# Routed attention and a gated feed-forward in one kernel: a unit's filler pieces start in its first gap instead of its second

## The chip, the cores and the metric

One Trainium2 chip, one core. The time is the device time of one execution, in microseconds (us); a lower one is better. Medians are over several executions. A profile shows one execution, and its span is about 1.8 us shorter than the time of that execution. The granted clock is the share of its full speed at which TensorE was allowed to run.

## The reference, cut to what matters

```python
# attention: 4 batches, 8 heads, 768 tokens, head size 64, 16 clusters per head
mask   = argmax(q_n @ c_n) == argmax(k_n @ c_n)       # a query sees the keys of its own cluster
attn   = softmax(where(mask, q @ k.T / 8, -1e9)) @ v
x      = attn as [3072 tokens, 512]
# feed-forward
xn     = x / sqrt(mean(x*x) + 1e-6) * rms_g
out    = (silu(xn @ w_gate) * (xn @ w_val)) @ w_out   # 512 -> 1536 -> 512
```

Inputs and output are float32.

## The kernel before

The work is cut into 8 *units* of 384 query tokens. A unit has 8 heads, and each head's scores come in three pairs of matmuls, so a unit has 24 *gaps*: the places after each score pair, where TensorE can do something else while ScalarE takes the exponential of the pair. The other work is cut into *pieces*, and a list of pieces is poured into the gaps by cost:

```python
    def attention(heads, fill, skip=0, hooks={}):
        gaps = [(u, h, i) for u, h in heads for i in range(UNITS[u][2])]
        total, done, n = sum(c for c, _ in fill), 0.0, 0
        for at, (u, h, i) in enumerate(gaps):
            scores(u, h, i)                       # 2 matmuls, then the exponential on ScalarE
            if i == (0 if (u, h) == (1, 0) else 1):
                for p in due:
                    pv(*p)                        # p*v of the head before: 18 small matmuls
                due[:] = [(u, h)]
            ...
            while n < len(fill) and at >= skip and done <= total * (at + 1 - skip) / (len(gaps) - skip):
                done += fill[n][0]
                fill[n][1]()
                n += 1
        for _, f in fill[n:]:
            f()
```

The pieces of a unit, in order: the last four gate/val pairs of the unit two before it; its own predecessor's normalisation (no TensorE work); nine output pieces with four transposes of the normalised tokens woven in; then eight gate/val pairs (0 to 7), and in units 2 to 5, woven among these, the preparation of a later *group* of four heads: eight f32 transposes, casts, and the cluster steps.

```python
        of["cl"] = cluster_products(...)          # TensorE, then a transpose on VectorE
        ...                                       # largest, same, back: VectorE only
   # a piece's chain
   gate: 4 matmuls -> tanh (ScalarE) -> (th+1)*gate (VectorE)    # its PSUM buffer is free after the last
   val:  4 matmuls -> 0.5*th*val (VectorE)
   transposes: 3 matmuls -> copy (ScalarE) -> casts (GpSimd and VectorE)
```

All of these write to one pool of three PSUM buffers; the scores have two of their own:

```python
    ps_s = pool("ps_s", 2, space=PSUM)    # score pairs, two banks each
    ps_a = pool("ps_a", 1, space=PSUM)    # p*v
    ps_g = pool("ps_g", 3, space=PSUM)    # everything else, tag "gen"
```

In the lines of the profile PE is TensorE, ACT ScalarE, DVE VectorE, POOL GpSimd and PEld TensorE's weight loads. A row gives its start, its duration and what was done; `[0.23 <-DVE th L432]` at its end means that the engine stood idle for 0.23 us before it, until an instruction of VectorE on line 432 was done. L333 is the score matmuls (tile s) and, on ScalarE, L337 their exponential (pT); L351 is p*v (acc) and L356 and L358 its division on VectorE; L423 is gate and val; L431 is the tanh, L432 and L436 the multiplies of gate and val; L448 is the output pieces; L208 and L214 are the f32 transposes and their copies; L227 is the casts; L244, L249, L253 and L271 are the cluster steps on VectorE.

The softmax here doesn't subtract the row's maximum and nothing guards it: scores larger than these inputs give would overflow.

## Time and profile before

| | kernel before |
|---|---|
| median time, first three runs (lowest, highest) | 346.39 us (346.12, 346.4) |
| span of the profile | 344.5 us |
| busy: TensorE / ScalarE / VectorE / GpSimd | 98% / 75% / 64% / 33% |
| length of unit 2; 3, 4 and 5; 6 (first score pair to the next unit's) | 42.16; 41.03 to 41.04; 36.37 us |
| unit 7 and the tail (first score pair to the end of TensorE's last matmul) | 74.78 us |

The lengths are differences of start times of the first score pair of each unit in the trace. A unit of 41.03 us holds some 40.5 us of TensorE work at its floor, as the prediction adds up. Unit 2 is longer because it holds one cluster product more (0.78 us, left over from an earlier group).

### The profile page before, as it was taken

How to read it: one execution, taken by the hardware profiler on the slowest of the kernel's cores; microseconds unless marked ns; L12 is line 12 of the kernel's file. 1: busy time of each engine (PE TensorE's matmuls, PEld its weight loads, DVE VectorE, ACT ScalarE, POOL GpSimd, SP SyncE). 2: the span in 40 equal slices, each digit the busy share in tenths (PEclk: the TensorE clock that was granted, in tenths of full speed). 3: DMA queues.
4: the chain of work that ended last, by engine and by line, in shares of the span. 5: the costliest groups of instructions: out<-in, count | busy, mean ns of one | idle time of the engine just before them, and what ended most of it. 6: DMA issues, size and time to landing. Idle time of an engine off the chain costs nothing.

```text
span 344.5 us, 7999 instructions
## 1 busy us (share of the span) xinstructions
PE 337.7 (98%) x3045; PEld 208.4 (61%) x3045; DVE 220.4 (64%) x540; ACT 259.4 (75%) x449; POOL 112.8 (33%) x225
## 2 busy tenths in 40 slices
PE   8999999999999999999999999999999999999996
PEld 4547657555765567565675656755566656655654
DVE  6999796975578626785367745686356645675330
ACT  5899979856888768886797777888778877764322
POOL 6999596234336205180132702435000000000000
DMA  8999979982450014400130010000100001001002
GB/s 266 381 209 219 263 147 232 149 275 87 147 159 17 30 62 149 139 22 35 61 94 2 23 63 33 0 9 17 63 32 0 2 33 61 2 1 64 30 2 91
DMA packets 27302, 31.62 MB, mean 92 GB/s; under 512 B 4480, under 2 KB 24320, under 8 KB 27264
## 3 DMA queue, kind: packets, MB, share of 16 engines
q1 hardware_dynamic: 18608, 25.02, 22.2%
q0 software_dynamic: 8368, 5.71, 10.2%
q8 instruction: 24, 0.39, 0.5%
q10 hardware_dynamic: 288, 0.39, 0.3%
q14 instruction: 14, 0.11, 0.1%
HBM read 28.35 MB, written 6.29 MB: 101 GB/s over the span
## 4 chain that ended last, share of the span: by engine, by line
PE 88%; ACT 5%; DVE 5%; issue 1%; POOL 0%; ACTq 0%; DVEq 0%; POOLq 0%
PE gate L423 17%; PE val L423 17%; PE o L448 17%; PE s L333 16%; PE acc L351 9%; PE tq L208 4%; ACT pT L337 4%; PE sc L241 3%; PE tx L396 1%; PE warm L117 1%; DVE pads L312 1%; DVE kext L317 1%; DVE qext L317 1%; PE o L459 1%; DVE scT L308 1%
## 5 line engine op out<-in xcount | busy, mean ns | idle before, releaser
L337 ACT ACTIVATE pT<-s,off 128x768 bf16<-128x768 f32 x192 | 170.6, 904 | 34.0 <-PE s L333 32.9
L333 PE MATMUL s<-qext,kext 80*128 80x384 bf16 x384 | 94.4, 327 | 1.8 <-ACT pT L337 1.1
L432 DVE SCALAR_TENSOR_TENSOR th<-th,gate 128x384 f32<-128x384 f32 x84 | 46.3, 552 | 51.8 <-ACT th L431 51.6
L423 PE MATMUL gate<-xnT,wg 128*128 128x384 bf16 x384 | 78.6, 326 | 0.1
L423 PE MATMUL val<-xnT,wv 128*128 128x384 bf16 x384 | 78.1, 326 | 0.0
L448 PE MATMUL o<-wo,gvT 128*128 128x512 bf16 x276 | 67.6, 379 | 0.0
L227 POOL CAST qext<-qkT 64x384 bf16<-64x384 f32 x64 | 35.3, 557 | 75.4 <-ACT qkT L214 35.9
L333 PEld LDWEIGHTS <-kext 80*128 80x128 bf16 x384 | 36.6, 98 | 31.4 <-issue 6.4
L431 ACT ACTIVATE th<-gate 128x384 f32<-128x384 f32 x84 | 41.2, 490 | 13.9 <-PE gate L423 13.5
L423 PEld LDWEIGHTS <-wv 128*128 128x128 bf16 x384 | 36.1, 97 | 25.5 <-issue 3.8
L423 PEld LDWEIGHTS <-wg 128*128 128x128 bf16 x384 | 35.9, 97 | 24.5 <-issue 3.3
L436 DVE SCALAR_TENSOR_TENSOR gvT<-th,val 128x384 bf16<-128x384 f32 x84 | 46.2, 550 | 6.2 <-PE val L423 1.6
L351 PEld LDWEIGHTS <-pT 128*128 128x128 bf16 x1152 | 43.4, 97 | 10.1 <-DVE x L358 1.1
L351 PE MATMUL acc<-vbf,pT 128*128 128x65 bf16 x1152 | 45.7, 193 | 0.6 <-ACT pT L337 0.2
L448 PEld LDWEIGHTS <-gvT 128*128 128x128 bf16 x276 | 25.7, 97 | 25.5 <-issue 0.6
L208 PE MATMUL tq<-ident_f,qk 128*128 128x128 f32 x192 | 30.8, 279 | 0.0
L214 ACT ACTIVATE qkT<-tq 128x384 f32<-128x384 f32 x57 | 26.9, 495 | 3.7 <-PE tq L208 3.2
L282 POOL DMA_DIRECT2D qext<-oh x40 | 19.1, 487 | 30.6 <-DVE oh L271 24.2
L397 DVE TENSOR_SCALAR xnT<-tx,gcol 128x384 bf16<-128x384 bf16 x28 | 10.6, 413 | 28.8 <-PE tx L396 28.8
L208 PEld LDWEIGHTS tq<-ident_f,qk 128*128 128x128 f32 x192 | 23.9, 144 | 6.6 <-ACT qkT L214 1.0
L451 ACT COPY o_sb<-o 128x512 f32<-128x512 f32 x23 | 13.5, 585 | 17.7 <-PE o L448 17.7
L282 POOL DMA_DIRECT2D kext<-oh x40 | 19.1, 485 | 9.6 <-DVE oh L271 9.6
(81 smaller groups left out, 247.2 us busy)
## 6 DMA issues: line engine op xcount, KB each, us to landing
qk<-in_q_dram SPq DMA_DIRECT2D x32, 192.0 KB, 3.8
vs<-in_v_dram SPq DMA_DIRECT2D x32, 192.0 KB, 4.0
out_dram<-o_sb SPq DMA_DIRECT2D x23, 256.0 KB, 2.0
qk<-in_k_dram SPq DMA_DIRECT2D x30, 192.0 KB, 4.1
wg<-in_moe_w_gate_dram POOLq DMA_DIRECT2D x4, 384.0 KB, 8.8
wv<-in_moe_w_val_dram POOLq DMA_DIRECT2D x4, 384.0 KB, 11.7
wo<-in_moe_w_out_dram POOLq DMA_DIRECT2D x3, 512.0 KB, 7.6
qext<-oh POOLq DMA_DIRECT2D x40, 12.0 KB, 1.6
```

What stands on the lines that cost most here:

```text
L208: nc.tensor.transpose(ps[:, i * P:(i + 1) * P], qk[:, part, 2 * i:2 * i + 2].rearrange("p t d -> p (t d)"), ident_f)
L214: nc.scalar.activation(to, ps, ACT.Copy, scale=by)
L227: on.tensor_copy(to, of)
L282: on.dma_start(out=ext[D:D + NC, h, e * UQ:(e + 1) * UQ], in_=put[g, m][32 * h + e * NC:32 * h + (e + 1) * NC])
L333: nc.tensor.matmul(ps[:, j, :w] if nt == HT else flat[:, j * w:(j + 1) * w], lhsT=cols(kext[g % 4][:KR, hh], g, kc // HT, kc % HT * P, (kc ...
L337: nc.scalar.activation(pT[u, h][:, n * i:n * i + n, :w], of, ACT.Exp, bias=off, scale=scale * ZS)
L351: nc.tensor.matmul(acc[:, h % 2, t], lhsT=pT[u, h][:, kc, t * P:(t + 1) * P], rhs=vbf[g % 4][:, hh, kc % HT * 2 + kc // HT], start=kc == 0 ...
L423: nc.tensor.matmul(ps, lhsT=w[:, c, f * P:(f + 1) * P], rhs=xnT[u][:, c, :n], start=c == 0, stop=c == CC - 1)
L431: nc.scalar.activation(th, ps, ACT.Tanh, scale=0.5)
L432: nc.vector.scalar_tensor_tensor(th, th, 1.0, ps, op0=ALU.add, op1=ALU.mult)
L436: nc.vector.scalar_tensor_tensor(gvT[u][:, f, :n], gates[u], 0.5, ps, op0=ALU.mult, op1=ALU.mult)
L448: nc.tensor.matmul(outs[u], lhsT=gvT[u][:, f, t * P:(t + 1) * P], rhs=wo[:, f], start=f == 0, stop=f == FC - 1)
```

## The change

The number at the end of the call is `skip`, the gaps at the start of a unit that get no piece. The intent is that TensorE should have something to do between the first two score pairs of a unit instead of waiting there for ScalarE.

```diff
-            attention([(u, h) for h in range(H)], fill + spread(ffn[CC:CUT], group(g) if g < NG else []), 1)
+            attention([(u, h) for h in range(H)], fill + spread(ffn[CC:CUT], group(g) if g < NG else []))
```

It holds for units 2 to 7. No piece is added or removed, and their order among themselves stays. The same total is now divided among 24 gaps and not 23.

## The prediction

> **What bounds the kernel now.** I read the page first (busy shares and the chain of work that ended last), then the list of waits, then the timeline of TensorE, engine by engine, around the places that the change touches.
>
> ```profile
> PE 337.7 (98%) x3045; PEld 208.4 (61%) x3045; DVE 220.4 (64%) x540; ACT 259.4 (75%) x449; POOL 112.8 (33%) x225
> ...
> PE 88%; ACT 5%; DVE 5%; issue 1%; POOL 0%; ACTq 0%; DVEq 0%; POOLq 0%
> ```
>
> TensorE is 98% busy and carries 88% of the chain. But a busy matmul row overlaps the next one, so I counted starts, not busy time. In the timeline a score pair starts 0.33 us before what follows it, a gate or val piece (4 matmuls) 0.65 us, an output piece (4 matmuls of 512 columns) 0.86 us, the 18 matmuls of a p*v product 0.55 us. One unit with a group (units 2 to 5) holds 24 score pairs, 8 p*v, 24 gate/val pieces, 9 output pieces, 12 bf16 transposes at 0.055, 8 f32 transpose triples at 0.33 and 2 cluster products at 0.78: 7.92 + 4.40 + 15.60 + 7.74 + 0.66 + 2.64 + 1.56 = 40.5 us. The double score pairs with which units 3, 4, 5 and 6 begin start at 107.23, 148.27, 189.30 and 230.34, so such a unit takes 41.04 us. Only 0.5 us of 41 is TensorE standing still. That is the main reading: reordering can move tenths, not microseconds.
>
> Where are those tenths? The waits of TensorE for ScalarE:
>
> ```profile
> PE s L333 <- ACT pT L337: 1.1, 4, 0.3
> ```
>
> and the start of the last unit in the timeline of TensorE (start, duration, what):
>
> ```profile
> 266.06 0.81 PE L423 MATMUL val<-xnT,wv 128*128 128x384 bf16 x4
> 266.71 0.49 PE L333 MATMUL s<-qext,kext 80*128 80x384 bf16 x2
> 267.47 0.49 PE L333 MATMUL s<-qext,kext 80*128 80x384 bf16 x2 [0.26 <-ACT pT L337]
> 267.79 0.71 PE L351 MATMUL acc<-vbf,pT 128*128 128x65 bf16 x18
> ```
>
> The second pair starts 0.76 us after the first where 0.33 would do: 0.43 us lost. The two score tiles alternate, so the pair needs the exponential of the pair two before it, and nothing was put between the pairs to give ScalarE time. At the other starts the loss is smaller:
>
> ```profile
> 107.23 0.88 PE L333 MATMUL s<-qext,kext 80*128 80x384 bf16 x4
> 107.95 0.71 PE L351 MATMUL acc<-vbf,pT 128*128 128x65 bf16 x18
> ```
>
> 0.72 us instead of 0.65: 0.07 us, the same at 148.27, 189.30 and 230.34. Unit 2 (65.07) loses 0.82 - 0.65 = 0.17 there and another 0.14 before a val piece at 68.86 that waits for a gen buffer (its gate started at 68.07, 0.79 before).
>
> **What the Trainium skill says.** "TensorE: Matmul & The Clock Gate", section "Wait — 56ns, not 53.3ns?": warm start-to-start is the columns over 2.4 GHz plus about 2.5 ns, 215.7 ns at 512; for 384 columns that works out to an estimated 162.5. The trace agrees: 0.86/4 = 215 ns and 0.65/4 = 162 ns, at a granted clock of 1.0. So the matmuls are at their floor. Same page, "Architectural detail: the array is 16× 32×32, not 1× 128×128": ScalarE and VectorE are strictly first in, first out. So a gate's tanh placed between two exponentials delays the second; the trace shows tanh and exponentials in program order throughout. "Perfetto Trace Analysis", "Identifying the Most-Contended Engine", warns against matmul busy time as a measure; here the busy rows (0.81 us for a piece that costs 0.65) agree. "ScalarE: Activation LUTs", "What ACT_TABLE_LOAD costs": back-to-back activations overlap by about 93 ns; here exponentials of 0.90 us follow each other at about 0.80.
>
> **The change part by part.** A unit has 24 gaps, one after each score pair. Pieces have a cost in the list; after a gap, pieces are issued while the running sum is within total*(gaps counted)/(gaps in all). The number 1 at the end of the call left the first gap empty: 23 gaps shared the work. Without it 24 do. The total is 27.62 with a group (units 2 to 5), so the quota goes from 27.62/23 = 1.20 to 1.15 per gap; units 6 and 7 have 23.82, from 1.036 to 0.993. No instruction is added or removed, and the order of the pieces among themselves is unchanged; only the score pairs and p*v products move against them.
>
> *Removed.* A gate and a val piece (1.30 us) now lie between the first two score pairs of units 2 to 7. That covers 0.43 + 4 x 0.07 + 0.17 = 0.88 us, and with an earlier gate in unit 2 probably the 0.14 too: 1.02 us, all on TensorE's path.
>
> *Moved at the border.* VectorE is behind there (the cluster steps of the old unit end at 109.46). With the durations of the trace: first gate at 107.56, val at 108.21, second pair 108.86, p*v 109.19, next gate 109.74, next val 110.39. That val needs the buffer of the first gate: its tanh would be done at about 109.25, VectorE's multiply at about 110.0. It fits with 0.4 us to spare. The remainder of the p*v (division, 0.7 us of VectorE) comes later by two multiplies and nobody waits for it. I count 0.
>
> *Moved within the unit.* Counting the quota by hand, the same pieces come out in each gap from gap 19 on, so the 0.16 us before the last val of units 2 to 5 (106.10 to 106.59 for a pair) stays. Between gaps 12 and 18 the grouping differs. Now the trace has, from the timeline of TensorE:
>
> ```profile
> 131.85 0.49 PE L208 MATMUL tq<-ident_f,qk 128*128 128x128 f32 x3
> 132.18 0.49 PE L333 MATMUL s<-qext,kext 80*128 80x384 bf16 x2
> 132.51 0.49 PE L208 MATMUL tq<-ident_f,qk 128*128 128x128 f32 x3
> 132.92 0.81 PE L423 MATMUL gate<-xnT,wg 128*128 128x384 bf16 x4
> ```
>
> 0.41 instead of 0.33 before the gate: 0.08 us. After the change both transposes of head 1 fall into gap 14 and gate 2 and val 2 into gap 15. Gap 14 then has 0.33 + 0.33 + 0.33 = 0.99 us of TensorE but about 0.79 + 0.38 + 0.38 = 1.55 us of ScalarE (exponential and two copies). Put on a clock that starts with the pair of gap 13: ScalarE gives the copies at 4.28 and 4.66, the tanh of gate 2 at 5.83; VectorE releases val 1 at 3.95, gate 2 at 6.43, val 2 at 7.2. TensorE wants gate 2 at 3.83 (waits about 0.15), gate 3 at 6.34 to 6.5 (fits or 0.1), the second transpose of head 2 at about 7.1 (waits about 0.1). Estimate 0.25 us in the place of 0.08, in four units: 4 x 0.17 = +0.7 us. Which of the three gen buffers a piece gets is not in the code, so this term runs from 0 to 0.6 a unit. Units 6 and 7 have no transposes and only light gaps: 0.
>
> Sum: -1.02 + 0.68 = -0.34 us, 346.39 to about 346.0.
>
> **The rivals.** First, the transpose gaps cost nothing, because ScalarE's idle time in the trace (75% busy) swallows the backlog: then the 0.08 go too and the time is 346.39 - 1.02 - 0.33 = 345.0. For it: the score tiles are double and gaps 17 and 18 with three transposes between them cause no loss today. Against it: there a p*v (0.55 us) follows and here none. Second, the gen buffers become the bound: VectorE's backlog at the border makes the early gate and val wait, or the transpose gaps wait 0.6 us; then 346.39 - 1.02 + 4 x 0.5 = 347.4, more if the border waits too. For it: VectorE runs without a break from 104.46 to 110.6; against it: the 0.4 us worked out above. Third, the normalisation of the previous unit now starts one gap earlier (gap 4 instead of 5 in units 2 to 5); it needs the last p*v of that unit, issued in gap 1, and lies about 5 us behind it instead of 7, while the division ends about 2 us behind it. Nothing: 0.
>
> **Range and chances.** The middle is 346.0; the ends of the two terms give 345.0 and 347.4, both less likely than the middle, and three runs of before spread by 0.28 us. Range 345.2 to 346.9. Two per cent is 6.9 us; the whole stall budget of the six units is about 3 us, so faster by 2% is out of reach (0.005), and slower by 2% would need a stall of over 1 us in every unit (0.01).
>
> **What would show it.** Right: at the start of units 3 to 7 a pair, a gate, a val, a pair, each at 0.33/0.65/0.65; the wait of the score matmuls for the exponential gone or down to 0.4 us or less; units 3 to 5 each between 40.9 and 41.4 us long; the unit before the last gains nothing except its border; last unit 0.4 us shorter. Wrong: a gate or val at the border that waits for VectorE, or a gap 14 to 17 in which TensorE loses more than 0.6 us, or an end (from the last score pair on) that is longer than now.

## More of the kernel before

The Trainium skill, "PSUM — Partial Sum Buffer", section "Specifications (TRN2)", gives 8 banks of 512 float32 per partition. Two score tiles of two banks, one p*v bank and three gen banks are all 8; no run here tries a ninth. A fourth gen buffer would have to be taken from another tile.

## The result, and the profile after

The changed kernel took 348.28 us (median of 4, 347.92 to 348.38), the kernel before beside it 346.38 us (4 runs). The ratio is 1.0055, with a 95% interval of 1.0037 to 1.0072: slower by half a per cent, and outside the predicted range. A ratio here and below is the mean time of one kernel's runs over that of the other's of the same rounds, so not quite the ratio of the medians.

The two lines of the page of the changed kernel that answer to those shown of before (busy time; chain by engine):

```profile
PE 338.8 (98%) x3045; PEld 208.4 (60%) x3045; DVE 221.3 (64%) x540; ACT 261.1 (75%) x449; POOL 112.8 (33%) x225
...
PE 85%; DVE 8%; ACT 5%; issue 1%; POOL 0%; ACTq 0%; DVEq 0%; POOLq 0%
```

The busy shares have hardly moved, but 3% of the chain has gone from TensorE to VectorE. The list of waits (who waits for whom: us in total, times, longest) says where to look:

```profile
PE val L423 <- DVE th L432: 0.9, 4, 0.2
```

This line is new: four times a val piece waits for the multiply that belongs to a gate. The wait of the scores for the exponential has gone from 1.1 us in four waits to 0.8 in three.

**The border is as predicted.** This is TensorE at the start of the last unit after the change (timeline: start, duration, what):

```profile
269.08 0.49 PE L333 MATMUL s<-qext,kext 80*128 80x384 bf16 x2
269.41 0.81 PE L423 MATMUL gate<-xnT,wg 128*128 128x384 bf16 x4
270.06 0.81 PE L423 MATMUL val<-xnT,wv 128*128 128x384 bf16 x4
270.71 0.49 PE L333 MATMUL s<-qext,kext 80*128 80x384 bf16 x2
```

Starts are 0.33, 0.65 and 0.65 apart: nothing waits, where 0.43 us were lost before. Unit 3 starts in the same way, without a wait.

**The loss is in units 2 to 5**, the units that prepare a group. From the starts of the first score pairs:

| unit | before | after | difference |
|---|---|---|---|
| 2 | 42.16 | 42.66 | +0.49 |
| 3 | 41.03 | 41.64 | +0.61 |
| 4 | 41.03 | 41.66 | +0.63 |
| 5 | 41.04 | 41.65 | +0.60 |
| 6 | 36.37 | 36.31 | -0.07 |
| 7 and tail | 74.78 | 74.35 | -0.43 |

(The differences are taken before rounding.) To find the places I took, for each matmul, the time to the next one's start, less the usual time for that shape. In each of units 2 to 5 two places stand out that the kernel before does not have, or has with a small wait only (0.08 before gate 2). The first, in unit 3:

```profile
131.44 0.81 PE L423 MATMUL val<-xnT,wv 128*128 128x384 bf16 x4
132.09 0.49 PE L333 MATMUL s<-qext,kext 80*128 80x384 bf16 x2
132.41 0.90 PE L208 MATMUL tq<-ident_f,qk 128*128 128x128 f32 x6
133.15 0.49 PE L333 MATMUL s<-qext,kext 80*128 80x384 bf16 x2
133.74 0.81 PE L423 MATMUL gate<-xnT,wg 128*128 128x384 bf16 x4
```

This is val 1, the two transposes of head 1, and gate 2. From the score pair at 133.15 to the gate are 0.59 us, where 0.33 would do: 0.26 lost. The two transposes take 0.74 from 132.41 to 133.15 where 0.66 would do; 0.055 of this is one wait inside the second of them, and I count it with the first place, 0.31 in all. Note that no idle time is printed before gate 2. The ends of matmul rows are modelled, 0.16 us later than the next start, so a short wait shows in the starts only.

The second place is val 4, 6.5 us later (0.23 us of idle time printed, but 0.39 lost: 1.04 from the transposes' start against 0.65):

```profile
138.23 0.81 PE L423 MATMUL gate<-xnT,wg 128*128 128x384 bf16 x4
138.88 0.49 PE L333 MATMUL s<-qext,kext 80*128 80x384 bf16 x2
139.21 0.82 PE L208 MATMUL tq<-ident_f,qk 128*128 128x128 f32 x6
140.25 0.81 PE L423 MATMUL val<-xnT,wv 128*128 128x384 bf16 x4 [0.23 <-DVE th L432]
```

In the kernel before the same pieces stand in another order against the scores and p*v:

```profile
137.74 0.81 PE L423 MATMUL gate<-xnT,wg 128*128 128x384 bf16 x4
138.39 0.82 PE L208 MATMUL tq<-ident_f,qk 128*128 128x128 f32 x6
139.04 0.49 PE L333 MATMUL s<-qext,kext 80*128 80x384 bf16 x2
139.37 0.71 PE L351 MATMUL acc<-vbf,pT 128*128 128x65 bf16 x18
139.92 0.81 PE L423 MATMUL val<-xnT,wv 128*128 128x384 bf16 x4
```

There a p*v (0.55 us) lay between the transposes and val 4. Now val 4 falls into gap 18, before it. These are the pieces of the gaps concerned, by the cost list (tr1a and tr1b are the two transposes of head 1, and so on; casts left out):

| gap | before | after |
|---|---|---|
| 13 (has a p*v) | val 0, tr0b, gate 1 | tr0b, gate 1, val 1 |
| 14 | val 1, tr1a | tr1a, tr1b |
| 15 | tr1b, gate 2, val 2 | gate 2, val 2 |
| 16 (has a p*v) | tr2a, gate 3 | tr2a, gate 3, tr2b |
| 17 | tr2b, val 3 | val 3, gate 4 |
| 18 | gate 4, tr3a, tr3b | tr3a, tr3b, val 4 |
| 19 (has a p*v) | val 4, gate 5 | gate 5 |

### The profile page after: what moved, and what is told of

It reads as the page before. It is cut to its first block, busy times and chain, and to the rows that moved or that the text cites. A ratio compares the mean times of both kernels' runs of the same rounds, so it can differ in the third digit from the quotient of the medians.

```text
span 346.5 us, 8001 instructions
## 1 busy us (share of the span) xinstructions
PE 338.8 (98%) x3045; PEld 208.4 (60%) x3045; DVE 221.3 (64%) x540; ACT 261.1 (75%) x449; POOL 112.8 (33%) x225
## 4 chain that ended last, share of the span: by engine, by line
PE 85%; DVE 8%; ACT 5%; issue 1%; POOL 0%; ACTq 0%; DVEq 0%; POOLq 0%
PE o L448 17%; PE val L423 17%; PE gate L423 17%; PE s L333 15%; PE acc L351 9%; ACT pT L337 3%; PE tq L208 3%; PE sc L241 3%; DVE th L432 1%; PE tx L396 1%; DVE gvT L436 1%; DVE kext L227 1%; PE warm L117 1%; DVE pads L312 1%; DVE kext L317 1%
```

## The experiments

My first theory: the border gains some 0.9 us, and two places in each of units 2 to 5 cost 0.31 and 0.39 us. The rival: the early pieces at the border themselves disturb VectorE, and what is seen later follows from that. All kernels ran in 4 to 6 timed runs beside the kernel before (medians of it 346.40 or 346.41). All outputs are right. Before the first score pair, profiles differ by up to 0.9 us from run to run (10.0 to 11.0 us), so I compare unit lengths beside the medians.

| run | median us | ratio to before (95%) | unit 3, us |
|---|---|---|---|
| kernel before | 346.4 | 1 | 41.03 |
| changed kernel | 348.28 | 1.0055 (1.0037 to 1.0072) | 41.64 |
| first gap alone | 345.37 | 0.9972 (0.9959 to 0.9984) | 40.97 |
| regrouped, first gap empty | 350.62 | 1.0122 (1.0109 to 1.0136) | 41.95 |
| val 4 after p*v | 346.27 | 1.0000 (0.9987 to 1.0013) | 41.26 |
| transposes apart | 347.89 | 1.0047 (1.0033 to 1.0060) | 41.65 |
| cast behind val 1 | 348.16 | 1.0041* (1.0013 to 1.0069) | 41.60 |
| casts behind gate 4 | 348.07 | 1.0040* (1.0010 to 1.0070) | 41.60 |
| val 4 and cast | 346.27 | 0.9993* (0.9965 to 1.0021) | 41.21 |
| val 4, cast, val 6 first | 346.22 | 0.9985* (0.9958 to 1.0012) | 41.16 |
| late gaps alone | 349.23 | 1.0080 (1.0067 to 1.0094) | 41.72 |
| val 4 and val 1 back | 345.68 | 0.9979 (0.9967 to 0.9992) | 41.01 |
| last two units only | 345.67 | 0.9979 (0.9967 to 0.9992) | 41.03 |
| first gap alone, val 6 first | 344.50 | 0.9947 (0.9935 to 0.9960) | 40.81 |

(* With the execution of 349.52 us among those of the kernel before, hence the wide intervals. Without it the ratios of the means would be 1.0051, 1.0049, 1.0003 and 0.9994, in this order; no conclusion below changes.)

### The two halves of the change

**First gap alone.** On the kernel before, the first two pieces go to gap 0; everything else keeps its gap.

```diff
-    def attention(heads, fill, skip=0, hooks={}):
+    def attention(heads, fill, skip=0, hooks={}, early=0):
 ...
+            for cost, piece in fill[:early] if at == 0 else []:
+                done += cost
+                piece()
+                n += 1
 ...
-  ... group(g) if g < NG else []), 1)
+  ... group(g) if g < NG else []), 1, early=2)
```

> The kernel before with one thing moved: the first gate and val piece of units 2 to 7 go to the first gap instead of the second, and all other pieces stay in their gaps of before. My theory now: the border gains what the prediction said (0.07 us in units 3 to 6, about 0.2 in unit 2, 0.43 in unit 7, together about 0.9 us) and the loss of the change lies only in the regrouping of later gaps. It expects 345.4 us (345.2 to 345.7), so about 0.9 us faster than before. The rival, that the early pieces at the border themselves cost (VectorE is behind there, their gen buffers come late), expects 347 us or more.

Measured 345.37, in the middle of the expected range. Units 3 to 5 are 0.06 us shorter than before, unit 2 by 0.30, unit 7 by 0.42. The border pieces gain and cost nothing here. Gap 1 is empty in this kernel, though, where the changed kernel fills it too; so the rival is out only together with the run "late gaps alone" below, which has the losses without any piece in the first gap.

**Regrouped, first gap empty.** The changed kernel, but gap 0 gets nothing and gap 1 four pieces.

```diff
-            while n < len(fill) and at >= skip and done <= ...
+            while n < len(fill) and at >= max(skip, hold) and done <= ...      # hold=1 for units 2 to 7
```

> The changed kernel with the first gap of units 2 to 7 left empty: the second gap takes four pieces, all later gaps are as in the changed kernel. Theory (the loss is two places in each of units 2 to 5: gate 2 behind two transposes loses about 0.31 us where 0.085 was lost before, and val 4 behind two transposes about 0.39): the border gain is missing, the loss is all there: 346.38 + 4 x (0.31 + 0.39 - 0.085) = 348.8 us (348.4 to 349.2), slower than the changed kernel. The rival (the border costs): 346.4, as before.

Measured 350.62, far off. Both places are there with the same 0.31 and 0.39, but the experiment made a third: four gate/val pieces in a row in gap 1, whose second val waits for its buffer (110.91 to 111.80 where 0.65 would do). That is 0.24 us in each of units 3 to 7 and 0.47 in unit 2, most of the 1.8 us above what I expected:

```profile
110.91 0.81 PE L423 MATMUL gate<-xnT,wg 128*128 128x384 bf16 x4
111.80 0.48 PE L423 MATMUL val<-xnT,wv 128*128 128x384 bf16 x2
```

So it does not measure the regrouping by itself. I repeated it in a cleaner form.

**Late gaps alone.** The kernel before up to gap 11, the grouping of the changed kernel from gap 12 on.

```diff
+            if at == 12:
+                skip = late          # 0 in units 2 to 5, else as it was
```

> The kernel before up to gap 11 of each unit (first gap empty, second gap with two pieces), then in units 2 to 5 the grouping of the changed kernel from gap 12 on (gap 12 takes one piece more to catch up). This is the regrouping without the crowded second gap that spoilt the first attempt. Theory: the two places cost what they cost in the changed kernel: 346.4 + 4 x (0.31 + 0.39 - 0.085) = 348.9 us (348.5 to 349.3). Rival, the earlier pieces of the first half also take part: 347.5 or less.

Measured 349.23, within the expected span. Unit 3 is 0.69 us longer than before, and in its starts the same three waits stand: 0.055 and 0.257 at gate 2, and 0.389 at val 4. With the first run this splits the change: the border -1.0 us, the regrouping +2.8 us. The sum is +1.8, and +1.9 was measured.

**Last two units only.** The first gap filled only where no group is prepared.

```diff
-  ... group(g) if g < NG else []))
+  ... group(g) if g < NG else []), int(g < NG))
```

> The changed kernel with the first gap filled only in units 6 and 7, which have no transposes; units 2 to 5 as before. Theory: the borders of units 6 and 7 gain 0.07 + 0.43 us and nothing is lost: 346.4 - 0.5 = 345.9 us (345.6 to 346.1). Rival, the whole change is bad at every unit: 346.4 or more.

Measured 345.67, as expected: units 6 and 7 keep their gain, units 2 to 5 are as before.

### The place before val 4

**Val 4 after p*v.** A little cost is moved from val 4 (piece 23 of the woven list) to the transpose before it, which pushes val 4 into gap 19 and moves nothing else.

```diff
+            work = spread(ffn[CC:CUT], group(g) if g < NG else [])
+            for i, cost in ((22, 0.15), (23, -0.15)) if g < NG else ():
+                work[i] = (work[i][0] + cost, work[i][1])
```

> The changed kernel with val 4 put back behind the p*v of gap 19 (0.15 of cost moved from val 4 to the transpose before it; no other piece changes its gap). Theory: the 0.39 us before val 4 go in units 2 to 5 and come back nowhere: 348.28 - 1.56 = 346.7 us (346.4 to 347.0). Rival: the wait is moved, not removed (gate 5 or the score pairs after it wait instead, because VectorE and ScalarE are simply behind there): 348.0 us or more.

Measured 346.27. Units 2 to 5 are each 0.39 us shorter than in the changed kernel, and no new wait appears: 1.56 us in all. The median fell by 2.0, slightly below what I expected; 0.25 us of the rest lies before the first score pair of the profile, where nothing was changed, so I take it for scatter. The wait was removed, not moved.

**Casts behind gate 4.** Why does val 4 wait? The trace names the multiply of gate 4 as what it waits for. The transposes hold the other two gen buffers, so val 4 needs the one of gate 4, and that comes free only after the tanh and the multiply. In the changed kernel two casts (138.90 to 139.61) stood before that multiply on VectorE. This run puts them behind it.

```diff
+                work[18:21] = [work[i] for i in (20, 18, 19)]      # gate 4, then the casts of head 2
```

> The changed kernel with the casts of head 2 issued behind gate 4 instead of before it, in units 2 to 5. Theory: val 4 must have the buffer of gate 4 because the two transposes took the other two, and that buffer comes free only after a matmul tail, a tanh of 0.49 and a multiply of 0.55 us in series; the tanh ends at 139.57 and the two casts at 139.61, so taking the casts out of the way gains at most 0.05 us a unit: 348.1 us (347.8 to 348.4). Rival, VectorE's casts (0.71 us) are what holds the multiply up: 348.28 - 4 x 0.39 = 346.7.

Measured 348.07, as the theory has it. From the timelines of TensorE, ScalarE and VectorE of this run:

```profile
138.21 0.81 PE L423 MATMUL gate<-xnT,wg 128*128 128x384 bf16 x4
...
140.19 0.81 PE L423 MATMUL val<-xnT,wv 128*128 128x384 bf16 x4 [0.19 <-DVE th L432]
```

```profile
139.06 0.49 ACT L431 ACTIVATE th<-gate 128x384 f32<-128x384 f32 x1 [0.29 <-PE gate L423]
```

```profile
139.58 0.56 DVE L432 SCALAR_TENSOR_TENSOR th<-th,gate 128x384 f32<-128x384 f32 x1 [0.62 <-ACT th L431]
```

Both other engines stood idle and took gate 4 as soon as they could. Still val 4 could start only 1.98 us after the gate's first matmul (138.21 to 140.19; 1.98 in units 2, 4 and 5 too). TensorE had 0.65 + 0.33 + 0.66 = 1.64 us of work in between. So what is left of the wait is the latency of the chain itself, which a less busy VectorE or ScalarE does not shorten. More TensorE work between the gate and the piece that takes its buffer covers it: with p*v in between there are 2.19 us, and nothing waits. A fourth buffer might too, which no run tried.

### The place before gate 2

This one took three attempts.

**Transposes apart.** First theory, from the prediction: two transposes in gap 14 overload ScalarE. So tr1b goes back to gap 15.

```diff
+            for i, cost in ((8, 0.3), (10, -0.3)) if g < NG else ():
```

> The changed kernel with the two transposes of head 1 in two gaps again (the second goes from gap 14 to gap 15, by 0.3 of cost moved from gate 2 to the first transpose; no other piece changes its gap). Theory: the 0.31 us before gate 2 shrink to the 0.08 of the kernel before: 348.28 - 4 x 0.23 = 347.4 us (347.1 to 347.7). Rival, the backlog of ScalarE makes another piece wait instead: 348.0 or more.

Measured 347.89: a miss. Gate 2 waits as long as before (0.66 us from the start of the transpose at 132.72, where 0.33 would do), and the profile names VectorE:

```profile
133.38 0.81 PE L423 MATMUL gate<-xnT,wg 128*128 128x384 bf16 x4 [0.17 <-DVE gvT L436]
```

**Cast behind val 1.** So VectorE. In the changed kernel its row runs almost unbroken from the division of the p*v of gap 13 to the multiply of val 1, whose buffer gate 2 gets:

```profile
130.63 0.20 DVE L356 RECIPROCAL inv<-acc 128x6 f32<-128x6 f32 x1 [0.32 <-PE acc L351]
130.86 0.56 DVE L358 TENSOR_TENSOR x<-acc,inv 128x384 f32<-128x384 f32 x1
131.51 0.51 DVE L227 CAST kext<-qkT 64x384 bf16<-64x384 f32 x1
132.16 0.56 DVE L432 SCALAR_TENSOR_TENSOR th<-th,gate 128x384 f32<-128x384 f32 x1
132.74 0.35 DVE L227 CAST kext<-qkT 64x384 bf16<-64x384 f32 x1
133.13 0.55 DVE L436 SCALAR_TENSOR_TENSOR gvT<-th,val 128x384 bf16<-128x384 f32 x1
```

The last row ends at 133.68 and gate 2 starts at 133.74. The cast at 132.74 belongs to no one in a hurry; this run issues it behind val 1.

```diff
+                work[6:8] = [work[i] for i in (7, 6)]
```

> The changed kernel with one cast of VectorE (second half of head 0's keys, a piece that costs TensorE nothing) issued behind val 1 instead of before it, in units 2 to 5. Theory now, after the transposes were parted and gate 2 waited as long as before: gate 2 waits for VectorE, whose row runs unbroken from the division of the p*v to val 1's multiply; the cast is 0.39 us of that row. Without it the multiply ends 0.39 earlier and the 0.26 us before gate 2 go: 348.28 - 4 x 0.26 = 347.2 us (346.9 to 347.6). Rival, ScalarE's two copies hold the buffer that gate 2 gets: 348.0 or more, as where the transposes were parted.

Measured 348.16: again a miss, but an instructive one. The wait of gate 2 is gone (its score pair at 133.38, the gate at 133.71). In gap 16 new ones stand:

```profile
135.88 0.53 PE L208 MATMUL tq<-ident_f,qk 128*128 128x128 f32 x3
136.31 0.81 PE L423 MATMUL gate<-xnT,wg 128*128 128x384 bf16 x4
137.04 0.55 PE L208 MATMUL tq<-ident_f,qk 128*128 128x128 f32 x3
137.42 0.49 PE L333 MATMUL s<-qext,kext 80*128 80x384 bf16 x2
```

0.43 where 0.36 is usual before gate 3, 0.73 where 0.65 is before tr2b, 0.38 where 0.33 is behind it: 0.20 us together, so a unit gains 0.05 and not 0.26. VectorE's wait had hidden another behind it.

**Val 4 and cast.** Both repairs on the changed kernel:

> Both repairs on the changed kernel: val 4 behind the p*v of gap 19, and the cast behind val 1. If the two places are independent and hold all of the loss, 346.5 (the repaired val 4 alone by its trace) - 4 x 0.26 = 345.4 us (345.0 to 345.7), the same as the kernel in which only the first gap was filled. If something else of the regrouping costs: 346 or more.

Measured 346.27, as with val 4 alone, and so a miss: moving the cast again brings waits into gap 16 (0.07, 0.08 and 0.055 us).

**Val 4 and val 1 back.** Revised theory: what changed here is that val 1 left gap 14. It is 0.65 us of TensorE work that asks nothing of ScalarE. Without it gap 14 has 0.99 us of TensorE work (a score pair, two transposes) against about 1.55 of ScalarE (an exponential, two copies), and both engines that empty buffers are late at once. This run puts val 1 back (and with it the cast before it, which costs TensorE nothing), and leaves the two transposes together.

```diff
+                work[5] = (work[5][0] + 0.3, work[5][1])        # gate 1
+                work[7] = (work[7][0] + -0.3, work[7][1])       # val 1 falls into gap 14
+                (val 4 moved as above)
```

> The changed kernel with val 4 behind the p*v of gap 19 and val 1 back in gap 14 (0.3 of cost moved from val 1 to gate 1), the two transposes of head 1 staying together. Theory, revised: the loss at gate 2 is there because val 1, 0.65 us of TensorE work that asks nothing of ScalarE, left gap 14, so that gap 14 has 0.99 us of TensorE against 1.55 us of ScalarE. With val 1 back the exponential of gap 14 starts 0.65 earlier and a buffer emptied by ScalarE is free for gate 2 in time: 346.3 - 4 x 0.25 = 345.3 us (345.0 to 345.7). Rival, VectorE's row is the only cause at gate 2: it is unchanged, so 346.0 or more.

Measured 345.68, within the expected span. TensorE's timeline:

```profile
130.98 0.81 PE L423 MATMUL val<-xnT,wv 128*128 128x384 bf16 x4
131.63 0.90 PE L208 MATMUL tq<-ident_f,qk 128*128 128x128 f32 x6
132.37 0.49 PE L333 MATMUL s<-qext,kext 80*128 80x384 bf16 x2
132.70 0.81 PE L423 MATMUL gate<-xnT,wg 128*128 128x384 bf16 x4
```

Gate 2 follows its score pair by 0.33: no wait. In the trace it now waits for a semaphore of ScalarE, and in the changed kernel for one of VectorE: it got the buffer of a transpose, emptied at 132.65 because the exponential before that copy had started earlier (131.24 instead of 132.61). The multiply of val 1 ended at 132.90 and would still have been 0.2 us late. No new wait follows, and the 0.08 in the transposes is left. In the changed kernel all three buffers were late: val 1's free at 133.68, those of the transposes at 133.89 and 134.27, where gate 2 could have started at 133.48. So parting the transposes cured nothing here and moving the cast a fifth; what removes the wait without a new one is val 1's TensorE time back between gap 14's pair and gate 2. Which buffer a piece gets is not in the code, and this run changed that too.

### A version that beats both

In all kernels so far the last val of units 2 to 5 waits 0.16 us for the buffer of val 6, whose multiply stands behind two cluster steps on VectorE. Issuing val 6 before these steps was tried twice.

```diff
+                work[31:34] = [work[i] for i in (33, 31, 32)]
```

**On the kernel with val 4 and the cast repaired:**

> The former kernel, and in units 2 to 5 also val 6 issued before the comparison and the back transpose of the clusters instead of behind them. In all kernels so far the last val piece of these units waits 0.16 us for the buffer of val 6, whose multiply stands in VectorE's row behind two cluster steps of about 0.5 us each. Theory: the 0.16 go, four times: 344.8 us (344.4 to 345.2). Rival, the two steps then push the next multiplies and a later piece waits instead: 345.2 or more.

Measured 346.22: a miss. The 0.16 are gone, but 0.11 appear in the next unit's gap 2 (a gate at 111.42, its val at 112.19). VectorE runs without a break across the border and the early pieces of the next unit come too fast for it.

**On the kernel with the first gap alone,** whose gap 1 is empty:

> The best kernel so far (only the first pieces moved to the first gap, 345.37) with val 6 issued before the two cluster steps in units 2 to 5. In the changed kernel this took the 0.16 before the last val but left 0.11 at the next unit's second val. Here gap 1 of the next unit has no pieces, so VectorE has time to catch up: 345.37 - 4 x 0.16 = 344.7 us (344.4 to 345.0). Rival, the wait comes back as there: 345.2 or more.

Measured 344.50, faster than the kernel before by half a per cent (ratio 0.9947) and the best of all. The border of units 2 and 3:

```profile
106.30 0.49 PE L333 MATMUL s<-qext,kext 80*128 80x384 bf16 x2
106.63 0.81 PE L423 MATMUL gate<-xnT,wg 128*128 128x384 bf16 x4
107.28 0.81 PE L423 MATMUL val<-xnT,wv 128*128 128x384 bf16 x4
107.93 0.49 PE L333 MATMUL s<-qext,kext 80*128 80x384 bf16 x2
```

Every start is 0.33 or 0.65 after the last one, and the last val of unit 2 (105.65, after a pair at 105.32) does not wait either. Unit 3 is down to 40.81 us, against 40.5 at the floor.

## Why the prediction was wrong

- **What bounds the kernel** was right: TensorE at its floor, and tenths to be won or lost. That the time would stay within 2% was right too.
- **"Removed", the border,** was right. Units 6 and 7 gained 0.07 and 0.43 as written, and the border alone measured -1.0 us against the -1.02 of the sum. In the changed kernel unit 2 keeps a 0.12 wait in its first gaps which the prediction thought would go.
- **"Moved at the border",** 0 us, was right: pair, gate, val, pair are at the written intervals.
- **"Moved within the unit" is the step that failed.** It says that the same pieces come out in each gap from gap 19 on. That is a miscount: gap 19 loses val 4 to gap 18. Of the gaps 12 to 18, where it sees a difference, only 14 to 17 were followed on a clock. So val 4, which moves from behind the p*v of gap 19 to before it, was never looked at, and cost 0.39 us in each of four units, 1.56 of the 2.3 us by which the prediction missed. The first rival even names the missing piece, the p*v that follows the transposes, as the reason why nothing waits there today, and does not see that the change takes val 4 out of its shelter.
- In the same step the gap-14 term was 0.25 us and measured 0.31 (0.26 at gate 2, 0.055 inside the second transpose). The size was nearly right, but partly by luck. The prediction told it as a backlog of ScalarE's two copies, and parting them changed nothing. Its clock was better than that story: it has VectorE release val 1 at 3.95, just after the 3.83 at which gate 2 wants a buffer. On the same clock (the pair of gap 13 starts at 129.55) the trace has that release at 4.13, so gate 2 waits 0.26 instead of 0.15. The two copies end at 4.34 and 4.72, close to the 4.28 and 4.66 foreseen. The waits of up to 0.1 that it foresaw at gate 3 and at tr2b did not come in the changed kernel; they came out, with 0.07 and 0.08, only when the cast was moved.
- Together a unit lost 0.31 + 0.39 = 0.70 us, more than the top of the term's own range (0.6). The prediction's sign for being right (units 3 to 5 at 41.4 us or less) failed with 41.64, but its sign for being wrong (over 0.6 us lost in a gap 14 to 17) did not come either: the larger loss lies in gap 18, just behind the gaps watched. The range given at the end was also narrower than the ends that the two terms gave.
- **The rival of the gen buffers** was the right one in kind: transpose gaps that wait for gen buffers. Its 347.4 was 0.9 short.
- Some 0.06 us of unit 3 is in none of these terms. By the starts it is in the transposes too: 0.03 inside the second one of head 0, in gap 13, and 0.03 between the two of head 1. No run was made for it.

## What to carry to other kernels

When a schedule pours pieces into slots by a running quota, changing one slot at the start re-divides all the others; list every piece that changes its slot, and for each ask whose buffer it takes and how much work now lies between. In this kernel, with three PSUM buffers for a gate, two transposes and a fourth piece, about 2 us have to lie between the start of the gate and that of the fourth (1.98 with both other engines idle), or TensorE waits. And a small wait that is taken away can uncover the next one: count starts over the whole unit, not only at the place repaired.

## What the Trainium skill lacked or had wrong

- "Perfetto Trace Analysis", section "Identifying the Most-Contended Engine", warns that matmul busy time misleads, but not that idle time does too (the page does call the end of a matmul estimated, in another section, without drawing this from it): the 0.26 us before gate 2 show no idle time at all, and the 0.39 us before val 4 show as 0.23. Start-to-start times against the shape's usual interval found both.
- No page that I read gives the turnaround of a PSUM buffer through two engines in series: 1.98 us here from a gate's first matmul, over a tanh (0.49) and a multiply (0.56), to the next matmul into the same buffer, with both engines idle beforehand.
- None of the figures that this text takes from the pages was contradicted by a trace here.
